# Re-ordering the first loads of a gated attention and GLU kernel: wk's second half on the ACT queue behind VectorE memsets

## The chip, the cores and the metric

The kernel runs on one core of one Trainium2 chip. Its time is that of the device in microseconds, from launch to end. The comparison is between medians of several executions of the kernel before and the kernel after; the kernel before has a median of 179.31 us over 7 runs (179.14 to 180.43). Profiles come from single executions; a profiled execution has a span (first to last instruction) and a time of its own, which is a little longer.

## What is computed

The input is `x` with 2048 tokens of 512 features, in bf16. Two blocks work on the same `x`, a linear attention with 32 heads of 16 features and a gated MLP (GLU) with 1376 hidden features. A sigmoid gate per token mixes them.

```python
def _A_ref(x, wqkv, wo):                       # linear attention
    q, k, v = split_heads(x @ wqkv)            # 32 heads of 16
    phi = lambda t: where(t > 0, t + 1, exp(t)) + 1e-6
    pq, pk = phi(q), phi(k)
    kv = einsum("bhsd,bhse->bhde", pk, v)
    z  = einsum("bhsd->bhd", pk)
    num = einsum("bhqd,bhde->bhqe", pq, kv)
    den = einsum("bhqd,bhd->bhq", pq, z)[..., None] + 1e-6
    return merge_heads(num / den) @ wo

def _B_ref(x, w1, w3, w2):                     # GLU
    return (silu(x @ w1) * (x @ w3)) @ w2

g = sigmoid((x * gate_w).sum(-1, keepdims=True))
out = g * _A_ref(x, wqkv, wo) + (1 - g) * _B_ref(x, w1, w3, w2)
```

The listing is cut and its helpers' names are shortened. `wqkv` holds the weights of q, k and v side by side; `wk` is its middle third, a 512 x 512 matrix.

## The kernel before

The 2048 tokens are cut into 16 tiles of 128 (index `t`) and 4 blocks of 512 (index `tb`). Features are cut into 4 chunks of 128 (index `kc`). Token-major copies of `x` lie in `x_sb`, feature-major ones in `xT`. A matmul that contracts over features needs `xT` as its stationary operand and a weight such as `wk_sb[:, kc, :]` as its moving operand, so `k` of one token tile takes four matmuls of 512 columns, one for each `kc`.

The stages follow each other on TensorE in an order written out by hand: first nine warm-up matmuls on constants (`emit_warm`, line 163), then transposes of the first two token tiles on TensorE (`emit_xT`, line 176; VectorE copies the first two chunks of each into `xT` at line 181, ScalarE the other two at line 183), then `k` for tiles 0 to 3 (line 186), then `k` for the others in turn with the accumulation of `phi(k)` against `x` (line 206), then `q`, then the GLU and the output blocks. `phi` uses ScalarE for the exponential (line 142) and VectorE for the rest (lines 144 and 147).

The first `k` matmuls don't go tile by tile. Line 379 sets their order as pairs of chunk and tile:

```python
    for kc, t in ((0, 0), (1, 0), (0, 1), (1, 1), (2, 0), (3, 0)):
        emit_k_mm(k0[t], t, kc)
```

Four matmuls thus use chunks 0 and 1 of `wk_sb`, and the fifth is the first that reads chunks 2 and 3. Tile 1's last two chunks, tile 2 and tile 3 come next. Tiles 0 and 1 get their `xT` from TensorE; tiles 2 and 3, and all later blocks, get theirs by a transposing DMA straight from memory (lines 89 and 93).

Loads are issued at the head of the program. All but one go out from SyncE (`dq`, SP's queue), one after the other: the first two token tiles of `x` (line 84), the second half of `wk_sb`, chunks 2 and 3 (line 86), the transposing load for tiles 2 and 3 (line 89), then for each further block a transposing load and a plain one (lines 93 and 98), then the other weights. The first half of `wk_sb`, chunks 0 and 1, goes out from ScalarE's queue (line 85). ScalarE then runs a small exponential, `pre` (line 88), whose purpose is to have the activation table loaded early.

Two buffers, `hr_bufs`, of 4 x 128 columns are set to zero by GpSimd at line 137. They hold the GLU's remainder columns later; the first write into them comes at 38.5 us. `ones_b`, a constant used at about 40 us, is set by VectorE at line 61.

On TensorE the order of the program is kept as written. On the other engines the framework orders instructions by its own priorities and places the semaphore waits that the data need.

Of the kernel before, what the change touches and what calls it, by code (L numbers as in the profile page):

```python
# [8 lines left out]
ACT = mybir.ActivationFunctionType  # L9
ALU = mybir.AluOpType  # L10
AX = mybir.AxisListType
ENG = mybir.EngineType
FP32 = mybir.dt.float32
BF16 = mybir.dt.bfloat16
# [3 lines left out]
def kernel(  # L18
# [12 lines left out]
    nc = tc.nc  # L31
    P = nc.NUM_PARTITIONS

    Bb, S, D = A_x.shape
# [7 lines left out]
    TPB = TB // P  # L42
# [9 lines left out]
    consts = ctx.enter_context(tc.tile_pool(name="consts", bufs=1))  # L52
# [11 lines left out]
    x_sb = consts.tile([P, NT, D], BF16, name="x_sb")  # L64
    xT = consts.tile([P, KC, S], BF16, name="xT")
    wk_sb = consts.tile([P, KC, D], BF16, name="wk_sb")
# [9 lines left out]
    wqkv_r = A_wqkv.rearrange("(kc d) n -> d kc n", d=P)  # L76
# [3 lines left out]
    dq = nc.sync  # L80
    TF = 2
    x_first = x2d[0 : TF * P, :].rearrange("(p j) d -> p j d", j=TF)
    out_first = out2d[0 : TF * P, :].rearrange("(p j) d -> j p d", j=TF)
    dq.dma_start(out=x_sb[:, 0:TF, :], in_=x_first)
    nc.scalar.dma_start(out=wk_sb[:, 0:2, :], in_=wqkv_r[:, 0:2, D : 2 * D])
    dq.dma_start(out=wk_sb[:, 2:4, :], in_=wqkv_r[:, 2:4, D : 2 * D])
    pre = consts.tile([1, 1], FP32, name="pre")
    nc.scalar.activation(out=pre[:], in_=nc.const_aps.tensor(0.0, [1, 1], FP32), func=ACT.Exp)
    dq.dma_start(
        out=xT[:, :, TF * P : TB], in_=x2d[TF * P : TB, :], transpose=True  # L90
    )
    for tb in range(1, NTB):
        dq.dma_start(
            out=xT[:, :, tb * TB : (tb + 1) * TB], in_=x2d[tb * TB : (tb + 1) * TB, :],
# [7 lines left out]
    with nc.allow_non_contiguous_dma(reason="one gate weight per partition and chunk"):  # L102
        dq.dma_start(
            out=wr_sb[:, :, 2 * FR : NR], in_=gate_w.rearrange("(kc d o) -> d kc o", d=P, o=1)
# [7 lines left out]
    for fcs in (slice(0, FC // 2), slice(FC // 2, FC)):  # L112
# [9 lines left out]
        out=bm, in_=bm, pattern=[[-Dh, HPC], [0, Dh]], compare_op=ALU.is_ge, fill=0.0,  # L122
# [3 lines left out]
        out=bm, in_=bm, pattern=[[Dh, HPC], [0, Dh]], compare_op=ALU.is_ge, fill=0.0,  # L126
# [4 lines left out]
    W_sb = consts.tile([P, KC, D], BF16, name="W_sb")  # L131
    z_sb = consts.tile([P, D], FP32, name="z_sb")
    omg = consts.tile([P, NT], FP32, name="omg")
    hr_bufs = []
    for i in range(2):
        hrb = consts.tile([P, TPB, P], BF16, name=f"hr{i}")
        nc.gpsimd.memset(hrb[:], 0.0)
        hr_bufs.append(hrb)

    def phi(dst, ps):  # L140
        e = work.tile([P, D], BF16, tag="phi_e", name="phi_e")
# [273 lines left out]
    for c in range(KC):  # L415
# [7 lines left out]
        out=kvT_sb[:], in0=kvT_ps[:],  # L423
# [65 lines left out]
```

## Time and profile before

| | us |
|---|---|
| median of 7 runs | 179.31 |
| lowest and highest run | 179.14, 180.43 |
| profiled execution, whole | 179.39 |
| its span | 177.5 |
| TensorE busy | 173.8 |
| VectorE busy | 117.7 |
| ScalarE busy | 65.9 |
| GpSimd busy | 63.3 |

The span starts with the first instruction on any engine. "SPq" and "ACTq" are the issuing of DMAs by SyncE and ScalarE, "PEld" is TensorE's loading of a stationary operand, which overlaps matmuls. A bracket such as `[0.21 <-DMA x_sb]` behind an instruction gives the time that its engine sat idle ahead of it and what ended that. A matmul's row lasts longer than the distance to the next one, since matmuls are pipelined: a 512-column matmul has a row of 379 ns, but the next one starts 0.216 us after it.

### The profile page before, as it was taken

How to read it: one execution, taken by the hardware profiler on the slowest of the kernel's cores; microseconds unless marked ns; L12 is line 12 of the kernel's file. 1: busy time of each engine (PE TensorE's matmuls, PEld its weight loads, DVE VectorE, ACT ScalarE, POOL GpSimd, SP SyncE). 2: the span in 40 equal slices, each digit the busy share in tenths (PEclk: the TensorE clock that was granted, in tenths of full speed). 3: DMA queues.
4: the chain of work that ended last, by engine and by line, in shares of the span. 5: the costliest groups of instructions: out<-in, count | busy, mean ns of one | idle time of the engine just before them, and what ended most of it. 6: DMA issues, size and time to landing. Idle time of an engine off the chain costs nothing.

```text
span 177.5 us, 2469 instructions
## 1 busy us (share of the span) xinstructions
PE 173.8 (98%) x884; PEld 83.5 (47%) x884; DVE 117.7 (66%) x203; ACT 65.9 (37%) x124; POOL 63.3 (36%) x71
## 2 busy tenths in 40 slices
PE   8999999999999999999999999999999999999993
PEld 3444444474445454444454544444545444444463
DVE  1586858898998637597876466878754668775000
ACT  3624224466433333333244333233434323241211
POOL 5197655958262323262003232710032328000000
PEclk9999999999999999999999999999999999999999
DMA  5999899931014011124000101230002022200011
GB/s 170 233 296 246 225 322 360 351 113 28 9 30 91 7 41 37 37 59 89 0 4 7 43 30 39 72 76 6 0 7 66 7 70 59 59 0 0 30 40 52
DMA packets 30253, 15.14 MB, mean 85 GB/s; under 512 B 20673, under 2 KB 30113, under 8 KB 30241
## 3 DMA queue, kind: packets, MB, share of 16 engines
q1 hardware_dynamic: 29968, 14.72, 30.8%
q10 hardware_dynamic: 272, 0.26, 0.4%
q8 instruction: 7, 0.11, 0.3%
q14 instruction: 6, 0.04, 0.1%
HBM read 8.42 MB, written 2.10 MB: 59 GB/s over the span
## 4 chain that ended last, share of the span: by engine, by line
PE 98%; DVE 0%; issue 0%; DVEq 0%
PE o_ps L357 20%; PE gate_ps L312 19%; PE up_ps L320 19%; PE o_ps L348 8%; PE XP L206 8%; PE q_ps L219 8%; PE k_ps L186 6%; PE r_ps L243 3%; PE k L186 2%; PE o_ps L352 2%; PE warm L163 2%; PE kvT_ps L418 1%; PE W_ps L440 0%; DVE o_out L366 0%; DVE xT L181 0%; PE xTp L176 0%
## 5 line engine op out<-in xcount | busy, mean ns | idle before, releaser
L312 PE MATMUL gate_ps<-xT,w_sb 128*128 128x512 bf16 x160 | 41.1, 379 | 0.0
L320 PE MATMUL up_ps<-xT,w_sb 128*128 128x512 bf16 x160 | 41.1, 379 | 0.0
L227 POOL TENSOR_TENSOR qz<-pq,z_sb 128x512 f32<-128x512 bf16 x16 | 18.5, 1161 | 59.6 <-DVE pq L147 58.4
L325 ACT ACTIVATE th<-gate_ps 128x512 bf16<-128x512 f32 x40 | 23.9, 597 | 37.9 <-PE gate_ps L312 37.5
L357 PE MATMUL o_ps<-w_sb,hT 128*128 128x512 bf16 (+2 forms) x180 | 37.5, 355 | 0.0
L327 DVE SCALAR_TENSOR_TENSOR gs<-th,gate_ps 128x512 bf16<-128x512 bf16 x40 | 27.3, 683 | 5.6 <-ACT th L325 5.3
L330 DVE TENSOR_TENSOR hT<-up_ps,gs 128x512 bf16<-128x512 f32 x40 | 27.6, 691 | 3.7
L144 DVE TENSOR_SCALAR phi_m<-phi_e 128x512 bf16<-128x512 bf16 x32 | 14.1, 440 | 21.6 <-ACT phi_e L142 21.4
L357 PEld LDWEIGHTS <-hT 128*128 128x128 bf16 x180 | 16.8, 97 | 17.9
L320 PEld LDWEIGHTS <-w_sb 128*128 128x128 bf16 x160 | 15.7, 98 | 18.9
L312 PEld LDWEIGHTS <-w_sb 128*128 128x128 bf16 x160 | 15.6, 98 | 18.6
L362 ACT ACTIVATE o_out<-o_ps,omg 128x512 bf16<-128x512 f32 (+2 forms) x17 | 11.1, 656 | 30.4 <-PE o_ps L357 30.4
L292 POOL TENSOR_TENSOR pqn<-pq,rden 128x512 bf16<-128x512 bf16 x16 | 16.5, 1055 | 14.0 <-DVE rden L285 11.7
L196 POOL TENSOR_TENSOR pks<-pks,pk_sb 128x512 f32<-128x512 f32 x15 | 17.5, 1168 | 7.4 <-DVE pk_sb L147 6.7
L348 PE MATMUL o_ps<-W_sb,pqT 128*128 128x512 bf16 (+2 forms) x72 | 16.8, 355 | 0.0
L230 DVE TENSOR_REDUCE den<-qz 128x32 f32<-128x512 f32 x16 | 11.0, 685 | 8.5 <-POOL qz L227 8.5
L219 PE MATMUL q_ps<-wq_sb,xT 128*128 128x512 bf16 x64 | 16.4, 379 | 0.0
L206 PE MATMUL XP<-pk_sb,x_sb 128*128 128x512 bf16 x64 | 16.3, 379 | 0.0
L142 ACT ACTIVATE phi_e<-k_ps 128x512 bf16<-128x512 f32 x12 | 7.2, 597 | 14.4 <-PE k_ps L186 14.4
L142 ACT ACTIVATE phi_e<-q_ps 128x512 bf16<-128x512 f32 x16 | 9.6, 597 | 7.8 <-PE q_ps L219 7.8
L186 PE MATMUL k_ps<-wk_sb,xT 128*128 128x512 bf16 x48 | 12.3, 379 | 0.0
L147 DVE SCALAR_TENSOR_TENSOR pq<-q_ps,phi_m 128x512 bf16<-128x512 f32 x16 | 11.1, 691 | 0.5
(59 smaller groups left out, 116.7 us busy)
## 6 DMA issues: line engine op xcount, KB each, us to landing
w_sb<-in_B_w_dram SPq DMA_DIRECT2D x6, 640.0 KB, 8.4
out_dram<-o_out SPq DMA_DIRECT2D x15, 128.0 KB, 1.9
x_sb<-in_A_x_dram SPq DMA_DIRECT2D x2, 512.0 KB, 4.6
x_sb<-in_A_x_dram SPq DMA_DIRECT2D x1, 768.0 KB, 5.0
wq_sb<-in_A_wqkv_dram SPq DMA_DIRECT2D x1, 512.0 KB, 6.6
wv_sb<-in_A_wqkv_dram SPq DMA_DIRECT2D x1, 512.0 KB, 6.9
wo_sb<-in_A_wo_dram SPq DMA_DIRECT2D x1, 512.0 KB, 9.9
wk_sb<-in_A_wqkv_dram ACTq DMA_DIRECT2D x1, 256.0 KB, 3.5
```

The source lines that it names most:

```text
L186: nc.tensor.matmul(k_ps[:], lhsT=xT[:, kc, t * P : (t + 1) * P], rhs=wk_sb[:, kc, :], start=(kc == 0), stop=(kc == KC - 1),)
L196: nc.gpsimd.tensor_add(pks[:], pks[:], pk_sb[:, t, :])
L206: nc.tensor.matmul(XP_ps[dc][:], lhsT=x_sb[:, t, dc * P : (dc + 1) * P], rhs=pk_sb[:, t, :], start=(t == 0), stop=(t == NT - 1),)
L219: nc.tensor.matmul(q_ps[:], lhsT=xT[:, kc, ts_tok], rhs=wq_sb[:, kc, :], start=(kc == 0), stop=(kc == KC - 1),)
L227: nc.gpsimd.tensor_tensor(out=qz[:], in0=st[tb, "pq"][:, tt, :], in1=z_sb[:], op=ALU.mult)
L312: nc.tensor.matmul(gate_ps[:], lhsT=w1_sb[:, kc, fsl], rhs=xT[:, kc, tok_sl], start=(kc == 0), stop=(kc == KC - 1),)
L320: nc.tensor.matmul(up_ps[:], lhsT=w3_sb[:, kc, fsl], rhs=xT[:, kc, tok_sl], start=(kc == 0), stop=(kc == KC - 1),)
L325: nc.scalar.activation(out=th[:], in_=gate_ps[:], func=ACT.Tanh, scale=0.5)
L327: nc.vector.scalar_tensor_tensor(out=gs[:], in0=th[:], scalar=1.0, in1=gate_ps[:], op0=ALU.add, op1=ALU.mult)
L330: nc.vector.tensor_tensor(out=st[tb, "hT"][:, fc, :], in0=up_ps[:], in1=gs[:], op=ALU.mult)
L348: nc.tensor.matmul(o_ps[:], lhsT=st[tb, "pqT"][:, c, tsl], rhs=W_sb[:, c, a:b], start=(c == 0), stop=False,)
L357: nc.tensor.matmul(o_ps[:], lhsT=st[tb, "hT"][:, fc, tsl], rhs=w2_sb[:, fc, a:b], start=False, stop=(fc == FC - 1),)
```

## The change

The first half of `wk_sb` moves from ScalarE's queue to SyncE's, as its second DMA. The second half moves from SyncE's queue to ScalarE's, and is issued there after the small exponential `pre`. VectorE zeroes the two `hr` buffers, in place of GpSimd, and then zeroes the second half of `wk_sb` twice. As the DMA of the second half writes the same bytes as these memsets, the framework makes ScalarE wait for the last of them before it issues the DMA. The order of ScalarE's and VectorE's instructions within this block is the written one.

```diff
-    dq.dma_start(out=x_sb[:, 0:TF, :], in_=x_first)
-    nc.scalar.dma_start(out=wk_sb[:, 0:2, :], in_=wqkv_r[:, 0:2, D : 2 * D])
-    dq.dma_start(out=wk_sb[:, 2:4, :], in_=wqkv_r[:, 2:4, D : 2 * D])
     pre = consts.tile([1, 1], FP32, name="pre")
-    nc.scalar.activation(out=pre[:], in_=nc.const_aps.tensor(0.0, [1, 1], FP32), func=ACT.Exp)
+    hr_bufs = [consts.tile([P, TPB, P], BF16, name=f"hr{i}") for i in range(2)]
+    with tc.manual_schedule(engines={ENG.Activation, ENG.DVE}):
+        for hrb in hr_bufs:
+            nc.vector.memset(hrb[:], 0.0)
+        for _ in range(2):
+            nc.vector.memset(wk_sb[:, 2:4, :], 0.0)
+        dq.dma_start(out=x_sb[:, 0:TF, :], in_=x_first)
+        dq.dma_start(out=wk_sb[:, 0:2, :], in_=wqkv_r[:, 0:2, D : 2 * D])
+        nc.scalar.activation(
+            out=pre[:], in_=nc.const_aps.tensor(0.0, [1, 1], FP32), func=ACT.Exp
+        )
+        nc.scalar.dma_start(out=wk_sb[:, 2:4, :], in_=wqkv_r[:, 2:4, D : 2 * D])
     dq.dma_start(
         out=xT[:, :, TF * P : TB], in_=x2d[TF * P : TB, :], transpose=True
     )
...
-    hr_bufs = []
-    for i in range(2):
-        hrb = consts.tile([P, TPB, P], BF16, name=f"hr{i}")
-        nc.gpsimd.memset(hrb[:], 0.0)
-        hr_bufs.append(hrb)
```

## The prediction

> **What bounds the kernel now.** I read the page's engine line and slices first, then the chain of waits in order of time for the first 9 us, then the timeline of that stretch by engine, then the DMA rows and the DMA rate by quarter microseconds.
>
> ```profile
> PE 173.8 (98%) x884; PEld 83.5 (47%) x884; DVE 117.7 (66%) x203; ACT 65.9 (37%) x124; POOL 63.3 (36%) x71
> PE   8999999999999999999999999999999999999993
> ```
>
> TensorE is busy in every slice, so only its holes can be won, and those of the edited stretch lie before 9 us. The chain of waits there (start, length, what):
>
> ```profile
> 0.84 3.04 PE warm L163 x9
> 3.88 0.25 PE xTp L176 x2
> 4.15 0.30 DVE xT L181
> 4.50 3.73 PE k L186 x16
> 8.23 0.86 PE XP L206 x4
> ```
>
> Four 512-wide matmuls take 0.86 us, so one takes 0.216. The 16 of `k` would need 3.45; the last one's tail (its 379 ns row minus 216) is 0.16; so 3.73 hides about 0.11 of waiting. From 8.23 on the pieces follow each other at 0.86 without a hole: a microsecond gained or lost before reaches the end in full. The timeline says where the holes are and when things are issued (start, length, engine, idle before and releaser):
>
> ```profile
> 0.80 0.45 ACTq L85 DMA_DIRECT2D wk_sb<-in_A_wqkv_dram  x1
> 0.81 0.40 SPq L84 DMA_DIRECT2D x_sb<-in_A_x_dram  x1
> 0.90 0.17 DVE L61 MEMSET ones_b<- 128x128 bf16 x1 [0.90 <-PEq L473]
> 1.26 0.41 SPq L86 DMA_DIRECT2D wk_sb<-in_A_wqkv_dram  x1
> 1.28 1.28 ACT L88 ACT_TABLE_LOAD   x1 [1.28 <-PEq L473]
> 1.73 1.32 SPq L89 DMA_TRANSPOSE xT<-in_A_x_dram  x1
> 2.58 0.20 ACT L88 ACTIVATE pre<-const-float32-0.0 1x1 f32<-1x1 f32 x1
> 3.10 2.87 SPq L93 DMA_TRANSPOSE xT<-in_A_x_dram  x1
> 3.82 0.45 PEld L176 LDWEIGHTS <-x_sb 128*128 128x128 bf16 x8 [0.21 <-DMA x_sb<-in_A_x_dram]
> 6.32 1.41 PEld L186 LDWEIGHTS <-xT 128*128 128x128 bf16 x8 [0.42 <-DMA xT<-in_A_x_dram]
> ```
>
> The last warm-up matmul (128 wide) starts at 3.57 in the timeline and runs at the slow clock (512-wide ones start 0.43 apart, a quarter of that is 0.11), so TensorE is free at 3.68 and waits for x until 3.82: hole one, 0.14. The third token tile's matmuls begin at 6.32, 0.11 after the first eight could have ended: hole two, for the transposed load. The 0.2 between the transposes and 4.50 is the VectorE copy, which stays. Landing times, from the page's DMA part (KB, us from issue to landing):
>
> ```profile
> wk_sb<-in_A_wqkv_dram ACTq DMA_DIRECT2D x1, 256.0 KB, 3.5
> x_sb<-in_A_x_dram SPq DMA_DIRECT2D x1, 256.0 KB, 3.0
> wk_sb<-in_A_wqkv_dram SPq DMA_DIRECT2D x1, 256.0 KB, 4.0
> ```
>
> So x lands at 0.81 + 3.0 = 3.8, wk's first half at 4.3, wk's second half at 1.26 + 4.0 = 5.26. The fifth `k` matmul, the first that reads the second half, is due at 4.50 + 0.86 = 5.36: today there is 0.10 of slack and no wait.
>
> ```profile
> 1.75:2.00 0.25, 0.25 (x2) 0.05 (x1) 0.00 (x0) 0.25 (x1) 0.25 (x2) 1.00 1.26 82
> 3.25:3.50 0.25, 0.25 (x3) 0.14 (x2) 0.00 (x0) 0.00 (x0) 0.00 (x0) 1.00 1.10 389
> 5.00:5.25 0.25, 0.25 (x3) 0.13 (x2) 0.00 (x0) 0.00 (x0) 0.00 (x0) 1.00 1.25 266
> ```
>
> The last figure of each row is GB/s. Nothing moves before 1.75, about 1.0 us after the first issue; then it ramps to 389. Adding the quarters, some 770 KB (the three loads are 786) are in by 4.5; from there the transposes run at 230 to 310.
>
> [...] ACT's load, issued with x, lands 0.5 after x, and SP's second load after both. [...]
>
> **The change part by part.**
> *Removed from GpSimd:* two hr memsets, 2 x 0.524. GpSimd idles from 3.0 to 7.7: nothing gained.
> *x alone in front:* ACT's 256 KB no longer compete with x. TensorE is free at 3.68 whatever x does, so the gain is between 0 and 0.14. I take 0.14.
> *wk's first half as SP's second DMA:* its bytes follow x's directly, as today's ACT load did; 524 KB are in at about 3.8 by the summed rates, and it should land near 4.3 (bounds 4.1 and 4.6, the latter from today's second SP load less 256 KB at 389 GB/s). It is due at 4.36. Up to 0.2 lost at the worst, covered if the second half is later still.
> *Transposes:* SP's third issue stays at 1.73, but 256 KB in front of it on the ring are gone; it starts up to 0.7 earlier, and hole two (0.11) goes.
> *ACT:* table load and `pre` (1.28 + 0.20) move ahead of the DMA issue and can end at about 0.80 + 1.5 = 2.3. Behind the DMA on ACT stands the copy of xT, first at 4.26: nobody suffers while the issue is over by 4.1.
> *VectorE:* after ones_b ends (1.07) come two hr memsets and two of wk's half. As words: [...] 2 x 0.30 + 2 x 0.565 = 1.73, end 2.80[...]. As bf16: 2 x 0.565 + 2 x 1.10 = 3.33, end 4.40. If they cost nothing, ACT still frees only at 2.3. I take 2.80[...].
> *The second half:* issued at 2.80 instead of 1.26. From issue to landing I take 3.0, x's row: the DMA engines are running by then, but transposes share them. Lower bound 2.25 (the page's 128 KB stores land in 1.9, plus 128 KB at 389 GB/s), upper 4.0 (the slowest wk row). It lands at 5.8 (5.05 to 6.8).
> *Sum:* the third tile starts 0.86 after the later of landing and due time (4.36 + 0.86 = 5.22). So the change of time is landing + 0.86 - 6.32 = landing - 5.46: +0.34 at 5.8; +1.34 at 6.8; and, with no stall, 5.22 - 5.46 = -0.24. The execution with this profile took 179.39 (span 177.5 and 1.9 around it), 0.08 over the median; 179.31 + 0.34 = 179.65.
>
> No gain beyond 0.24 is to be had: everything after 6.32 was already without holes.
>
> **The rivals.** A measurement of this kernel tells 0.3%, 0.54 us, from no change.
> *Late behind the transposes (slower).* Place: the fifth `k` matmul. [...] SP is issuing 4.2 us of transposes (1.73 to 5.97) and their small packets. For it: [...] the 3.5 of today's ACT row; its first bytes, too, came after x's. Against it: the transposes' bytes are spread over time[...]. It decides from a landing at 6.0, 3.2 after the issue. At 3.7 it lands at 6.5: +1.04, 180.35.
> *Memsets at 2-byte width.* Issue at 4.40, landing 7.4, +1.94: 181.25. VectorE's copy of xT would wait to 4.4 as well and ACT's to 4.85, both inside the same stall. For it: ones_b's rate[...].
> *The holding back does nothing, or landing is quick.* The issue at 2.3 to 2.8 and 2.3 to 2.4 to landing give 4.6 to 5.2: no stall, -0.24, 179.07. The 3.0 to 4.0 of all three loads speak against it; that those began on DMA engines standing still speaks for it.
>
> **How the numbers follow.** Short stall (-0.1 to +0.54): 0.38. No stall (about -0.24): 0.18. Late behind the transposes: 0.28. Memsets at 2-byte width: 0.12. A gain over 0.54 by something that I don't see: 0.04. Within 0.3% is 0.38 + 0.18 = 0.56, slower 0.28 + 0.12 = 0.40, faster 0.04. The range goes from 178.95 (a little under the no-stall case) to 181.0 (all of the late case, +1.34, and the lower edge of the slow memsets); it leaves out some 0.04 below and 0.1 above.
>
> **What would show it.** The four VectorE memsets ending near 2.8 (wrong at 4.4); the ACT-queue issue right behind; x's transposes starting near 3.68; the first `k` matmul near 4.36; then a wait of about 0.6 for wk ahead of the fifth; and no wait at the third tile. The forecast is wrong if the second half lands after 6.0, if wk's first half is what TensorE waits for, or if the span changes behind 9 us.

## The result and the profile after

The changed kernel is slower. Its median is 182.96 us over 13 executions (180.56 to 185.17), that of the kernel before 179.70 over 32; the comparison gives a ratio of 1.0114 with an interval of 1.0087 to 1.0140. It leaves out executions that lie over 1.5% above the kernel's own lowest, five of the 13, which is why the ratio is under that of the two medians (1.018). The forecast was 179.65, no change, with a range from 178.95 to 181.0.

The profiled execution took 181.03 with a span of 179.3, against 179.39 and 177.5. The chain of waits of the changed kernel says where the 1.8 us are (start, length, what):

```profile
1.67 0.50 DVE wk_sb L90
2.17 0.16 issue
2.33 0.50 DVE wk_sb L90
2.82 0.02 issue
2.85 4.36 DMA wk_sb<-in_A_wqkv_dram
7.21 0.04 issue
7.25 2.75 PE k L189 x12
10.00 0.86 PE XP L209 x4
```

Where the chain of the kernel before went through TensorE and one copy on VectorE, it now goes through VectorE's memsets, of which the last two are shown, and then for 4.36 us through one DMA. The load lands at 7.21; the twelve matmuls that need it follow at once. Its timeline has the rest (start, length, engine, idle before and releaser):

```profile
1.07 0.55 DVE L88 MEMSET hr<- 128x256 uint32 x2
...
2.85 0.42 ACTq L96 DMA_DIRECT2D wk_sb<-in_A_wqkv_dram  x1
...
3.09 3.76 SPq L101 DMA_TRANSPOSE xT<-in_A_x_dram  x1
...
3.67 1.06 PE L179 MATMUL xTp<-ident,x_sb 128*128 128x128 bf16 x8
...
4.53 1.15 PE L189 MATMUL k<-wk_sb,xT 128*128 128x512 bf16 x4
...
7.25 2.75 PE L189 MATMUL k<-wk_sb,xT 128*128 128x512 bf16 x12 [1.57 <-DMA wk_sb<-in_A_wqkv_dram]
```

The memsets go out as 4-byte words and end at 2.82. TensorE stands still from 5.68 to 7.25. Behind that nothing is lost: 12 matmuls at 0.216 are 2.59, plus the tail of 0.16, which is 2.75. The rate of the DMA engines in the same stretch, last figure in GB/s, first the kernel before, then the changed one:

```profile
4.50:5.50 1.00, 1.00 (x5) 0.50 (x6) 0.17 (x1) 0.42 (x2) 0.00 (x0) 1.00 1.25 272
5.50:6.50 1.00, 1.00 (x6) 0.31 (x4) 0.00 (x0) 0.49 (x2) 0.00 (x0) 1.00 1.29 266
7.50:8.25 0.75, 0.75 (x5) 0.31 (x4) 0.72 (x3) 0.50 (x1) 0.53 (x1) 1.00 0.21 50
```

```profile
4.50:5.50 1.00, 1.00 (x7) 0.47 (x5) 0.29 (x1) 0.61 (x2) 0.00 (x0) 1.00 0.95 186
5.50:6.50 1.00, 0.18 (x1) 0.00 (x0) 0.00 (x0) 0.00 (x0) 0.00 (x0) 1.00 1.22 182
6.50:7.25 0.75, 0.00 (x1) 0.00 (x0) 0.00 (x0) 0.00 (x0) 0.00 (x0) 1.00 1.19 187
7.25:8.25 1.00, 1.00 (x5) 0.48 (x5) 0.00 (x0) 0.37 (x1) 0.00 (x0) 1.00 1.28 290
```

While the ACT queue's load and the transposing loads are both under way, the two together move about 185 GB/s; as soon as the load has landed, the transposes alone move 290. The last row of the kernel before was there to be read ahead of the prediction: where a plain load follows a transposing one (7.50 to 8.25), the rate falls to 50 for 0.75 us.

One thing is not in this profile. Each execution lists TensorE's mean granted clock, the share of full speed that it was allowed, and six of the 13 have 0.991, with times from 182.96 to 184.02; the others, at 0.998 to 1.000, have a median of 181.54. Experiment 7 comes back to this. The slowest of all, 185.17, is among the others (1.000); no profile caught it, and it stays unexplained.

### The profile page after: what moved, and what is told of

Read it like the earlier page. It is cut to its first block, busy times and chain, and to the rows that moved or that the text cites. A ratio compares the mean times of both kernels' runs of the same rounds, so it can differ in the third digit from the quotient of the medians.

```text
span 179.3 us, 2471 instructions
## 1 busy us (share of the span) xinstructions
PE 174.0 (97%) x884; PEld 84.2 (47%) x884; DVE 119.3 (67%) x207; ACT 66.0 (37%) x124; POOL 62.3 (35%) x69
## 4 chain that ended last, share of the span: by engine, by line
PE 94%; DMA 2%; DVE 1%; issue 0%; DVEq 0%
PE o_ps L360 19%; PE gate_ps L315 19%; PE up_ps L323 19%; PE o_ps L351 8%; PE q_ps L222 8%; PE XP L209 8%; PE k_ps L189 6%; PE r_ps L246 3%; DMA wk_sb<-in_A_wqkv_dram 2%; PE o_ps L355 2%; PE k L189 2%; DVE wk_sb L90 1%; PE kvT_ps L421 0%; PE W_ps L443 0%; DVE hr L88 0%
```

## The experiments

Two theories stood at the start. *Issue time*: the load takes its 4.4 us from whenever it is issued. *Queueing*: it gets its bytes after those of the loads that the sync queue issued before it, and shares with those issued after. The first experiments undo parts of the change.

### 1 and 2: no holding back; ACT's load first of all

```diff
-        for _ in range(2):
-            nc.vector.memset(wk_sb[:, 2:4, :], 0.0)
```

> Leaves out the two VectorE memsets of wk's second half; all else as in the changed kernel. Its load should be issued from the ACT queue at about 2.3 us (after the exponential) and not at 2.85. Issue-time theory (landing is the issue plus the 4.36 us measured): lands at 6.7, total about 0.5 us under the changed kernel. Queue theory (the load gets its first bytes only when the transposing load issued before it is through, at about 4.6): lands at 6.9 to 7.2 as now, total within 0.3 us of the changed kernel.

In the second, the load also stands ahead of the exponential:

```diff
+        nc.scalar.dma_start(out=wk_sb[:, 2:4, :], in_=wqkv_r[:, 2:4, D : 2 * D])
         nc.scalar.activation(
...
-        nc.scalar.dma_start(out=wk_sb[:, 2:4, :], in_=wqkv_r[:, 2:4, D : 2 * D])
```

> No memsets of wk, and the ACT queue issues wk's second half as its very first instruction (0.80 us), before any transposing load is issued. Both theories: lands by 4.0 to 5.2, no wait at the fifth k matmul, time equal to the kernel before or up to 0.25 us under it. If it still lands after 6, the ACT queue itself is at fault, against both.

Both were slower than the kernel before: 1.0088 (1.0049 to 1.0128) and 1.0063 (1.0031 to 1.0095). The timeline of ScalarE without the memsets holds the first surprise:

```profile
0.80 1.28 ACT L91 ACT_TABLE_LOAD   x1 [0.80 <-PEq L474]
0.86 0.43 ACTq L94 DMA_DIRECT2D wk_sb<-in_A_wqkv_dram  x1
2.09 0.20 ACT L91 ACTIVATE pre<-const-float32-0.0 1x1 f32<-1x1 f32 x1
```

The DMA stands behind the exponential in the program, yet it is issued at 0.86, while the table load runs. Table load and exponential hold nothing back, although the change was described as issuing the load after the exponential; the memsets were the only hold. So both experiments test the same thing: the second half issued at about 0.8. It then landed in time (4.0 and 3.6 us after its issue, at 4.9 and 4.4), but it went ahead of wk's first half, which the sync queue issues second. That one landed 4.4 and 4.2 after its issue, and the first `k` matmul had to wait for it until 5.66 and 5.49. My expectation for the second had overlooked this: it looked at the half that moved and not at the one that it overtook. The halves are needed in order, and a load issued 0.4 us ahead on the other queue landed ahead. What was issued with it counts, too: the first half was issued at 1.26 in the changed kernel as well and landed 3.1 us later there. That fits queueing; for the second half the issue-time theory isn't refuted yet. The order isn't strict, though: in the kernel before, ACT's load was issued 0.01 us ahead of x and landed 0.5 us behind it.

The executions of both kernels fall into two groups: without the memsets four have spans of 178.2 to 178.9 and three of 180.4 to 180.6. The second kernel's profile is one of the upper group. From its chain of waits:

```profile
1.26 4.18 DMA wk_sb<-in_A_wqkv_dram
5.44 0.04 issue
5.49 5.63 PE k L187 x16
```

The 16 `k` matmuls took 5.63 where they took 3.73 before: they stand 0.43 apart for most of it. In this profile the 2 us are thus a clock that stays low longer: the trace's first clock entry, the rise to full speed, comes at 9.6 us here, against 4.2 in the profile without the memsets, which is one of the lower group. Ahead of that entry the granted clock reads 1.00 although the matmuls stand 0.43 apart, so the mean of 1.000 doesn't show a late rise. That the other executions of the upper group are the same is likely, but not shown.

### 3: all three loads on the sync queue

The memsets of wk's second half are left out here too:

```diff
         dq.dma_start(out=wk_sb[:, 0:2, :], in_=wqkv_r[:, 0:2, D : 2 * D])
+        dq.dma_start(out=wk_sb[:, 2:4, :], in_=wqkv_r[:, 2:4, D : 2 * D])
...
-        nc.scalar.dma_start(out=wk_sb[:, 2:4, :], in_=wqkv_r[:, 2:4, D : 2 * D])
```

> No memsets of wk; x, wk's first half and wk's second half all go out from the sync queue in this order, ahead of the transposing loads; ACT only runs its exponential. Issued at about 1.7, the second half should land near 4.6 to 5.3; due at 5.3. Both theories: no wait, the kernel before or up to 0.25 us under it; the transposing loads are issued 0.45 us later, so tile 2 may wait up to 0.4 us, which would make it equal or 0.2 us slower.

> All three first loads on the sync queue once more, for a second profile. In the first profile no load was waited for and the whole loss was k matmuls 0.43 apart until 6.7 us. If the moment of the clock's rise is by chance, this profile may have it near 4, and then the third tile (due at 6.1) waits for its transposing load, which was issued 0.5 us later than in the kernel before, by 0.1 to 0.4 us.

Ratios of 1.0052 (1.0034 to 1.0070) and 1.0042 (1.0022 to 1.0063): half a per cent slower. The first profile has no wait for any load in the head; its chain of waits is TensorE alone:

```profile
0.84 3.04 PE warm L164 x9
3.88 0.85 PE xTp L177 x8
4.74 4.33 PE k L187 x15
```

Here x landed early and the work began at 3.67, but all at the low clock, which rose only at 6.7. In the second profile the clock rose at 4.7, and there the second half landed 4.3 us after its issue, at 6.03, and cost 0.60, and tile 2's transposing load another 0.25. So the order "x alone, then both halves" on a single queue gains nothing either: what x gains runs into the low clock, and both wk's second half and the transposing loads come later than in the kernel before.

### 4: which loads does it wait behind?

The first two transposing loads, or block 1's alone, become plain loads of the same bytes:

```diff
     dq.dma_start(
-        out=xT[:, :, TF * P : TB], in_=x2d[TF * P : TB, :], transpose=True
+        out=xT[:, :, TF * P : TB],
+        in_=x2d[TF * P : TB, :].rearrange("(p j) (a b) -> p (j a) b", j=2, a=2),
     )
...
+        if tb == 1:
+            dq.dma_start(
+                out=xT[:, :, tb * TB : (tb + 1) * TB],
+                in_=x2d[tb * TB : (tb + 1) * TB, :].rearrange("(p j) d -> p j d", j=4),
+            )
```

> The changed kernel with the first two transposing loads (tiles 2 and 3, and block 1) made plain loads of the same bytes into the same places; k and q of tiles 2 to 7 are then computed from tokens that are not transposed. If the transposes are what the ACT queue's load waits for and shares with, it lands about 3.0 us after its issue (near 5.9) and the stall falls from 1.95 to about 0.6 us. If any traffic issued earlier on the sync queue does it, it lands at 6.5 to 7.2 as now.

> The changed kernel with block 1's transposing load alone made a plain load of the same bytes (k and q of tiles 4 to 7 are then computed from tokens that are not transposed). The ACT queue's load still stands behind the transposing load of tiles 2 and 3, so its bytes begin near 4.6. If what stretches it is sharing with transposes, the two queues together now move 340 GB/s or more where they moved 110 to 240, and it lands by 6.6. If it is the sharing as such, at equal parts, the rate together stays under 250 and it lands at 7 or later.

The chains of waits have the load's time from issue to landing, first with both plain, then with block 1's alone:

```profile
2.85 5.02 DMA wk_sb<-in_A_wqkv_dram
```

```profile
2.85 5.69 DMA wk_sb<-in_A_wqkv_dram
```

So transposes are not needed for it to be late: plain loads of the sync queue in front and beside do it as well (block 2's transposing load, issued behind them, moved its first packets after 8 us). That speaks against transposes as such being the cause. They do matter for the rate. With both plain, the engines moved 153 GB/s from 4.5 to 5.25 and then 348 from 5.5 to 7.0, so that for most of the time the load shared a good rate; with the transposing load of tiles 2 and 3 still in front, 132 from 5 to 6 and 162 from 6 to 7. That load landed only at 7.5, so the two were under way together in both stretches. With both plain the order of issue was broken once: block 1's plain load of 512 KB was issued 0.4 us ahead of the ACT queue's 256 KB and landed at 8.8, behind it at 7.9.

### 5: the load by itself

A one-column copy on GpSimd reads wk's second half and writes into the target of a transposing load, which then has to wait. In a first form the framework stayed free to order the sync queue's loads:

```diff
+    nc.gpsimd.tensor_copy(xT[:, 0, TF * P : TF * P + 1], wk_sb[:, 2, 0:1])
```

> The changed kernel, but a one-column GpSimd copy that reads wk's second half stands ahead of the first transposing load, so that the sync queue issues nothing after wk's first half until the second half has landed. The ACT queue's load then has no other load beside or ahead of it but x and wk's first half, both nearly through. If its lateness is the queueing behind and beside the sync queue's loads, it lands 2.3 to 2.6 us after its issue at 2.85 (5.2 to 5.4) and the fifth k matmul waits at most 0.1; tile 2 then waits for its late transposing load instead, to about 9. If lateness belongs to the ACT queue or to an issue at that time, it lands near 7.2 again.

The framework moved the held load behind those of blocks 1 and 2 and issued block 1's transposing load (512 tokens) third in its place, so this run tells the opposite of what was meant: with twice the transposes in front and more beside, the load landed 6.1 us after its issue. In the second form the copy is the same, and the sync queue's order is kept as written (its block made part of the manual schedule):

> The changed kernel, with a one-column GpSimd copy that reads wk's second half ahead of the first transposing load, and the sync queue's order kept as written, so that after x and wk's first half it issues nothing until the second half has landed. If the lateness is that of standing behind and beside transposing loads, the second half lands 2.3 to 2.6 us after its issue at 2.85 (5.2 to 5.4), at 300 GB/s or more. If it belongs to the ACT queue or to the late issue itself, it lands at 6.5 or later. Tile 2 waits for its transposing load until about 9 in either case.

Now nothing is in the way. The ACT queue's issue, and its time to landing:

```profile
L96 ACTq DMA_DIRECT2D wk_sb<-in_A_wqkv_dram x1: 418/418/418, 2.8 to 2.8; - x1
...
DMA to landing us min/median/max: 2.8/2.8/2.8
```

It lands 2.8 after its issue, at 5.66, with 266 GB/s from 4.5 to 5.25, a little slower than expected. The same instruction on the same queue at the same time: neither the ACT queue nor the late issue makes it late. This is one profile, but 1.6 us under the lowest of the changed kernel. The issue-time theory falls; queueing stands.

### 6: behind or beside

One more kernel, profiled twice, holds the sync queue, in the order written, only after the transposing load of tiles 2 and 3, so that the load stands behind that one and has no other beside it:

```diff
+    nc.gpsimd.tensor_copy(xT[:, 0, TB : TB + 1], wk_sb[:, 2, 0:1])
```

> The changed kernel, with the sync queue held after the transposing load of tiles 2 and 3 until wk's second half has landed (a one-column GpSimd copy reads it and writes block 1's first column of xT). The ACT queue's load then stands behind one transposing load but has none beside it later. If the share of standing behind is what its first bytes show (4.6 against 3.9), it lands near 6.3 to 6.5, 3.5 after its issue, and what is over that in the changed kernel (0.8 to 2.3 us) comes from block 1's transposes beside it. If it lands at 7.2 or later, standing behind one transposing load does it all.

> The same kernel once more, since the landing in the changed kernel differs between executions by 1.5 us: within 0.4 us of the other look if the beside part is what varies, up to 1.5 us apart if the behind part does.

The time from issue to landing in the two profiles:

```profile
DMA to landing us min/median/max: 4.7/4.7/4.7
```

```profile
DMA to landing us min/median/max: 4.1/4.1/4.1
```

And one, without the memsets of wk, puts the load into the same place in line, but on the sync queue itself, where it was issued at 3.10:

```diff
+    dq.dma_start(out=wk_sb[:, 2:4, :], in_=wqkv_r[:, 2:4, D : 2 * D])
     for tb in range(1, NTB):
```

> No memsets of wk; its second half goes out on the sync queue, behind the transposing load of tiles 2 and 3 and ahead of block 1's: the place in line that the ACT queue's load took in the changed kernel (first bytes near 4.6), but on one ring with the transposes. If two rings with transposes on one of them are what stretches the load (7.2, 8.2 and 8.7 in three profiles), it lands near 5.9 and the time falls to about 0.5 us over the kernel before (0.3%). If the place in line alone does it, it lands at 7 or later and the time stays 1.5 us or more over the kernel before.

| | in front | beside | landing after issue, us |
|---|---|---|---|
| held altogether | x, first half | nothing | 2.8 |
| held after tiles 2 and 3 | one transposing load | nothing | 4.7, 4.1 |
| changed kernel, two profiles, and its filled form (experiment 7) | the same | block 1's transposing load | 4.4, 5.3, 5.8 |
| same place on the sync queue | the same | the same, behind it in its own queue | 4.5 |
| block 1's made plain | the same | block 1's plain load | 5.7 |
| both made plain | plain loads | plain loads | 5.0 |

Company of one transposing load, issued 1.1 us ahead, costs 1.3 to 1.9 us, more than I expected of it (0.7). Against the mean of these two, 4.4, the next one beside adds nothing in one profile, 0.9 in another and 1.4 in the third. So the load in front is the larger part, and the one beside may be what varies most; two profiles against three are an indication and no more, and the two held ones, 0.6 us apart, lie between the two cases of their expectation. Nor is it pure waiting behind: the transposing load in front itself landed at 6.8 and 6.3 in the held kernel and at 7.9 and 8.3 in the repeat and the filled form, against 5.3 in the first profile of the changed kernel. The two loads slow each other. The same place on the sync queue landed at 7.6, as late as on the ACT queue, and gave 1.0070 (1.0040 to 1.0101), against 1.0114 and, in a repeat of the changed kernel, 1.0097 (1.0052 to 1.0143): the intervals overlap, so whether the second queue costs anything of its own stays open. Why the engines move about 185 GB/s and at times less where plain and transposing loads meet, against 290 and 348, isn't shown either.

The cost of extra bytes there was measured by itself. To the kernel of experiment 3, which waits for no load on the ACT queue, a further 256 KB load was added on that queue, into a tile that nobody reads:

```diff
+    spare = consts.tile([P, 2, D], BF16, name="spare")
...
+        for _ in range(2):
+            nc.vector.memset(spare[:], 0.0)
...
+        nc.scalar.dma_start(out=spare[:], in_=wqkv_r[:, 2:4, D : 2 * D])
```

> All three first loads on the sync queue, and a further 256 KB load of the same weights on the ACT queue, issued near 2.85 behind two memsets of its target, a tile that nobody reads: extra bytes beside the transposing loads, with no one waiting for them. If a plain load on the ACT ring slows the transposing loads beside it, the rate between 5 and 7 us falls under 200 GB/s (285 without), the transposing loads of tiles 2 and 3 or of block 1 come 1 us later or more, and TensorE waits for them: 0.5 to 2 us over the same kernel without the extra load. If the two rings only share bandwidth, the transposes move up by the extra 256 KB, 0.9 us at the most.

1.0219 (1.0143 to 1.0295), against 1.0052 and 1.0042 without it: some 3 us, more than the 0.5 to 2 expected, for a load that would take 0.75 us of the engines at the 348 GB/s of experiment 4 (an estimate). Not all of it is the transfer: three of the four executions have a mean clock of 0.981 or 0.991, and the one at 1.000 took 181.91, which is 1.5 us over the median without the load. The transposing load of tiles 2 and 3 landed 8.3 us after its issue, against 4.5 and 4.9. The window rows with the extra load show why (last figure GB/s):

```profile
5.00:6.00 1.00, 1.00 (x4) 0.35 (x3) 0.00 (x0) 0.15 (x1) 0.00 (x0) 1.00 1.46 146
6.00:7.00 1.00, 0.10 (x2) 0.05 (x1) 0.00 (x0) 0.00 (x0) 0.00 (x0) 1.00 0.78 141
...
8.00:9.00 1.00, 0.00 (x0) 0.00 (x0) 0.76 (x2) 0.67 (x2) 0.00 (x0) 0.97 1.38 115
9.00:10.00 1.00, 0.00 (x0) 0.00 (x0) 0.96 (x3) 0.00 (x0) 0.61 (x1) 0.50 1.51 70
```

The last row also shows the clock, third figure from the right: it fell to 0.50 while TensorE stood idle.

### 7: the idle stretch and the clock

The changed kernel was run again, and once with the idle stretch filled with dummy matmuls:

```diff
     for kc, t in ((0, 0), (1, 0), (0, 1), (1, 1), (2, 0), (3, 0)):
+        if (kc, t) == (2, 0):
+            emit_warm(*[P] * 16)
         emit_k_mm(k0[t], t, kc)
```

> The changed kernel once more, for a second profile and more times. wk's second half lands at 7.2 within 0.5 us if the queueing sets it, and the gap before the fifth k matmul is then about 1.7 at the fast clock; the rest of what this execution takes over 181 us is matmuls that stand 0.43 apart.

> The changed kernel with 16 more warm-up matmuls of 128 columns between the fourth and the fifth k matmul, where TensorE waits for wk's second half; the result is the same. They take 0.9 us at the fast clock and 1.7 at the slow one, inside a wait of 1.7. If the changed kernel's spread (180.6 to 185.2) comes from a slow clock that the idle stretch prolongs, its upper end falls away and the median comes down to about 181.2. If the spread is that of the landing time alone, median and spread stay, within 0.3 us.

> The kernel before once more, for a second profile. The loads land within 0.3 us of the first profile (x 3.8, wk 4.3 and 5.3). If the moment at which TensorE's clock rises differs from execution to execution, the first k matmuls stand 0.43 apart here where they stood 0.216 apart; the total then lies up to 1.3 us over 179.1.

The repeat gave 180.76, 182.00, 184.05 and 185.45. The filled kernel gave 182.46, 182.47, 182.80 and 183.25, 1.0173 (1.0148 to 1.0199): the upper end is gone, but so is the lower, and the median isn't at 181.2. Its profile says why: the load landed later still, 5.8 us after its issue, and even there TensorE idled 1.45. Its four executions all have a clock of 1.000, where eight of the 17 of the changed kernel and its repeat have 0.991 or 0.981; with four executions that is a hint. The repeat's load, expected at 7.2 within 0.5, landed at 8.18. From the chain of waits of the repeat and of the filled kernel:

```profile
2.84 5.33 DMA wk_sb<-in_A_wqkv_dram
8.18 0.04 issue
8.22 2.75 PE k L189 x12
```

```profile
2.85 5.81 DMA wk_sb<-in_A_wqkv_dram
8.65 0.04 issue
8.69 2.32 PE k L189 x10
```

In these two profiles the clock did not fall, and the sum of the prediction holds: 8.18 - 5.46 = 2.72 and 8.65 - 5.46 = 3.19, and the spans are 180.3 and 180.8, 2.8 and 3.3 over 177.5. The spread of the changed kernel is to this extent that of the landing. Their timelines show one more wait, for wk's first half, ahead of the first `k` matmul; the first two lines are the repeat's, the last is the filled kernel's:

```profile
4.50 1.02 PE L189 MATMUL k<-wk_sb,xT 128*128 128x512 bf16 x4 [0.18 <-DMA wk_sb<-in_A_wqkv_dram]
8.22 2.75 PE L189 MATMUL k<-wk_sb,xT 128*128 128x512 bf16 x12 [2.70 <-DMA wk_sb<-in_A_wqkv_dram]
```

```profile
5.28 1.02 PE L189 MATMUL k<-wk_sb,xT 128*128 128x512 bf16 x4 [0.65 <-DMA wk_sb<-in_A_wqkv_dram]
```

The other part of the spread shows in the one-queue kernel of experiment 6, whose profiled execution took 183.25 where its others took 180.46 to 181.52. Its stall, and its window rows (granted clock third from the right):

```profile
7.61 4.44 PE L187 MATMUL k<-wk_sb,xT 128*128 128x512 bf16 x12 [2.00 <-DMA wk_sb<-in_A_wqkv_dram]
```

```profile
5.50:7.50 2.00, 0.12 (x1) 0.00 (x0) 0.00 (x0) 0.00 (x0) 0.00 (x0) 1.00 1.32 139
7.50:8.25 0.75, 0.64 (x3) 0.31 (x3) 0.00 (x0) 0.00 (x0) 0.00 (x0) 0.88 1.28 290
8.25:11.25 3.00, 3.00 (x8) 1.06 (x7) 1.88 (x4) 1.63 (x3) 0.87 (x2) 0.50 0.82 239
11.75:13.00 1.25, 1.25 (x8) 0.54 (x7) 1.22 (x3) 0.60 (x1) 0.39 (x1) 1.00 1.26 273
```

TensorE idled 2.00 us; at 8.07, when it was at work again, the clock fell to half for 3.41 us, and twelve matmuls took 4.44 us in place of 2.75: 1.7 us on top of the wait. Half the clock for 3.41 of 181 us lowers the mean by 0.009, to 0.991, the figure of six of the changed kernel's 13 executions, and their median, 183.45, lies 1.9 us over that of the others. That the six are the same event is an inference from this figure; no profile of the changed kernel itself caught it.

Four more profiles have a fall ahead of the kernel's end: both forms of experiment 5, block 1's load made plain, and the extra load. In all five the trace has it 3.41 us after the clock's rise, and the clock stays at half for 3.41, 3.41, 6.83, 6.83 and 10.24 us, which are one, two and three times 3.41; their mean clocks are 0.991, 0.991, 0.981, 0.981 and 0.973. In these five, TensorE idled 1.86 to 2.24 us of the 3.41 between rise and fall; in the profiles without a fall, at most 1.88 of the 3.41 after the rise (the first profile of experiment 3 has no clock entry and is left aside). The repeat's stall is longer, 2.70 us, but it lies across the end of that stretch: with the 0.18 ahead of it, 1.80 us of idling fall before that end and 1.07 behind it. So what seems to count is the idle time within one stretch of 3.41 us, and not the length of the stall. The two ranges touch, and this was read from the traces afterwards; no experiment set out to test it.

The second profile of the kernel before has its loads where the first has them and a span of 177.5 as well; there the clock rose half a microsecond later, and the `k` matmuls began 0.05 later and met no hole at tile 2.

No kernel tried here is as quick as the one before.

## Why the prediction was wrong

*The bound and the sum: right.* The only place that counts is the fifth `k` matmul, and landing minus 5.46 gave 1.75 for a landing at 7.21; the span grew by 1.8. It held in two further profiles.

*VectorE: right, the end by 0.02.* Memsets in word form, end forecast at 2.80 and measured at 2.82; the terms differ a little (0.272 for 0.30, 0.485 and a wait of 0.17 for 0.565), so the end is in part luck: the two memsets of 512 words were 0.16 quicker than forecast, and the wait, which the forecast didn't have, makes up for it. The terms were the author's estimate; no row of the kernel before shows a memset in words. The rival with memsets at 2-byte width is out.

*ScalarE: wrong, without effect.* The forecast had the DMA issue held until 2.3 by table load and exponential; without the memsets it goes out at 0.86.

*x alone in front: half right.* It landed 2.5 after its issue in place of 3.0, and TensorE took it up at 3.67 without a wait. But the 0.14 were not gained: the eight transposes ran at the low clock and took 1.06 in place of 0.62, so `k` began at 4.53, not at 4.36. What started earlier here ran at the low clock and took 0.44 longer.

*wk's first half: right in one profile of three.* In the first it landed at 1.26 + 3.1 = 4.4 (4.3 forecast) and nobody waited. In the repeat, where the transposes ran at the fast clock, the first `k` matmul waited 0.18 for it, and in the filled kernel, where it landed 4.0 after its issue, 0.65; the forecast had named such a wait as a sign of being wrong. *Tile 2's wait: right*, it is gone, though in the repeat its load landed only at 7.9 and was covered by the stall.

*The second half: this is the step that failed.* "From issue to landing I take 3.0, x's row", with 4.0 as the upper bound. It took 4.36, and 5.3 and 5.8 in two more profiles. The 3.0 is right for a load with nothing in its way, 2.8 measured. The bound failed since each of the three rows that it came from had only plain loads, and at most two, ahead of it; none had a transposing load in front. The forecast named the rival that came true, late behind the transposes, with its place, and gave it 0.28; but it priced it at 3.7, and its range, 1.69 over 179.31, ended at a landing of 7.15, just under the earliest that a profile of the changed kernel shows, 7.21. Its reason, that SP is issuing transposes at that time, isn't all that the runs show: with plain loads in front and beside, the load was late as well, 5.0 us after its issue. A hint that such company is dear stood in the kernel before, where a plain load behind a transposing one begins with 0.75 us at 50 GB/s; it isn't enough for a price.

*A stall priced at its own length: wrong in part.* The sum adds the wait for the second half and nothing else. That a stall costs no more was the author's assumption, which no row of the kernel before shows. It held in the three profiles of the changed kernel and its filled form, whose clock did not fall. In the one-queue kernel the clock fell to half for 3.41 us after a stall of 2.00 us, and the price was another 1.7 us. So a stall of 2 us in the first 10 us carried, in part of the executions, nearly its own length again.

## What to carry to other kernels

A load's price holds for its place in line. Before one is delayed or moved to another queue, list the bytes issued ahead of it and soon after it on every queue, since in the profiles here they delayed it whichever queue they were on (landing 4.1 to 6.1 us after its issue, against 2.8 by itself), and look for a row that shows the load in that company; a row from quiet company is the lower bound, not the middle. Loads that are needed in order are best issued in that order, and those needed first ahead of any transposing load, as in the kernel before: when the second half went out 0.4 us ahead of the first, TensorE waited for the first until 5.66 and 5.49. A stall that TensorE has not had before can cost more than its length: here 2.00 us of waiting cost 1.7 more at half the clock.

## What the runs showed of the hardware that was not expected

- A DMA on ScalarE's queue did not wait for the activation written ahead of it: issued at 0.86, the table load running until 2.08 and the activation at 2.09.
- A 256 KB load on one queue took 2.8 us by itself (one profile), 4.1 and 4.7 behind a transposing load of another queue, 4.4 to 5.8 with a further one beside it.
- Plain and transposing loads under way together moved about 185 GB/s and at times 70 to 160, where plain ones alone moved 348 and transposes alone 290. An extra 256 KB in that stretch cost about 3 us, 1.5 in the one execution whose clock didn't fall.
- TensorE's clock rose at moments from 3.7 to 6.7 us, and in one profile at 9.6, though TensorE's first 3.5 us are the same instructions in all; with matmuls 0.43 apart in place of 0.216, each microsecond at the low clock costs half of one.
- It fell again ahead of the kernel's end in five profiles, 3.41 us after the rise in each, for one, two or three times 3.41 us, where TensorE had idled 1.86 to 2.24 us of the 3.41; in the others it had idled at most 1.88 and the clock did not fall.
